# An attention and expert kernel: a reduction, a cast, a key order and the first expert's product are moved

## The chip, the cores and the metric

The kernel runs on one core of a Trainium2 chip. The core has a matmul engine (PE, with its weight loads as PEld), a vector engine (DVE), a scalar engine (ACT), a general engine (POOL), and a sync engine (SP) that issues nearly all DMAs. Each engine works through its own list in order; semaphores hold an instruction until what it reads is there and what it overwrites is free. The metric is the time of one execution on the device, in microseconds, the median of several runs.

## The reference, cut to what matters

```
# u, v: 8 x 2496 x 256, z: 8 x 2496 x 64, float32
scores = (1 / S) * z @ z.T                  # for each batch, symmetric
attn = maximum(scores, 0) ** 2              # symmetric too
x = (u * (attn @ v)).reshape(19968, 256)
logits = x @ w_gate                         # 8 experts
e_of = argmax(logits, axis=1)
gate_w = softmax(logits)[e_of]
for e in range(8):                          # at most 80 rows for each expert
    tok = the 80 rows of largest gate_w among those with e_of == e
    h = maximum(x[tok] @ w1[e], 0)          # w1[e]: 256 x 1024
    out[tok] = gate_w[tok] * (h @ w2[e])    # w2[e]: 1024 x 256, other rows are 0
```

## The kernel before

**Staging.** The kernel goes through 8 batches `b`. A batch is cut into 5 chunks `qc` of 512 queries (the last has 448), and a chunk goes in ten steps `r`, each for a pair of key tiles of 128 rows. A fifth number in a tile name is the pair's first key tile: `al_5_3_12` is batch 5, chunk 3, key tiles 12 and 13. `order(b, qc)` gives the pairs of a chunk. The loop over all steps is written out by hand: what each engine does, and when, is the order of the calls.

**A pair.** A number is carried as a high and a low part, so a product takes three matmuls. Half of the score matrix is computed and the other half is mirrored. For a computed pair PE makes the scores `s` (line 407), ACT takes Relu and Square (lines 409, 410, tile `a`) and casts the high part `ah` (line 114), and DVE subtracts to the low part `al` (line 58) and transposes `a` into a tile `x` (line 316), which SP writes to memory as `y` (line 326). A mirrored pair is read back from there as `blk` (line 343); ACT casts `ah` (line 387) and DVE subtracts `al`. The last pair of a chunk lies on the diagonal; half of it is mirrored through `xd`, `yd` and `md` (lines 352, 360, 369; cast in line 422). `attend_pair` then multiplies `ah` and `al` with the values `vt` into two accumulators `acc`: 24 matmuls on half arrays (line 444). The scores or casts of a pair are issued two steps ahead of its `attend_pair` (`LOOK = 2`).

**The end of a chunk.** ACT copies the accumulators out (`take`, line 516). Over the next chunk's steps DVE adds halves, multiplies with `u` (line 524) and cuts off low parts; PE makes the gate logits `pl` (line 602), and DVE sums them to `lg` (line 609, `chunk_sum`). The steps of this are the table `CHAIN` in `finished`. `pl`, and the count tables `wp` (lines 839 to 841, `blocks`) for the first two batches, use the one buffer with tag `m`, so `wp` can begin only when DVE has read `pl`. The step 9 that calls `blocks` is also the one at which `chunk_sum` is called.

**The next batch's values.** `prep_vh` casts a quarter or so of the values of the next batch to the high part of `vt`, on ACT, at the five places of `V_HIGH`; the last of them is in the last step of a batch.

**The end.** In the last batch the rows for the experts are fetched and spread (`x_at`: `fetch_x`, `spread_x`, line 799), and the first two experts' weights are loaded and split (`LOADS`, `SPLITS`). After the last attention product come the last rows' sums and logits (`chunk_x_last`, lines 538 to 540, `chunk_logits_last`, lines 549 to 553), the gate, and a feed-forward stage of eight experts. For expert i it transposes the rows (`xp_i`, line 1302; split to `xTh_i`, `xTl_i`), multiplies with w1 (`hp_i`, line 1322), takes Relu (line 1325), transposes the result (line 1337; split to `hTh_i`, `hTl_i`) and multiplies with w2 (`op_i`, line 1352).

Of the kernel before, what the change touches and what calls it, by code (L numbers as in the profile page):

```python
# [8 lines left out]
F32 = mybir.dt.float32  # L9
# [10 lines left out]
P = 128  # L20
# [5 lines left out]
def attn_moe_kernel(ctx, tc, zT, uT, v, wg, w1, w2, out, seq, cap):  # L26
# [39 lines left out]

    const = ctx.enter_context(tc.tile_pool(name="const", bufs=1))
    dram = ctx.enter_context(tc.tile_pool(name="dram", bufs=1, space=DRAM))
    NV, NW, NR = 6, 2, 5
    NA = 4  # L70
    NX = 4
    SQ = 32
# [67 lines left out]
    def prep_vh(b, g, raw, e0):  # L140
        vt = vpool.tile([P, QT, 2, D], F32R, tag="vt", name=f"vt_{b}_{g}")
        cp(e0, vt[:, :, 0], raw)
        v_t[b, g] = vt
# [145 lines left out]
    def order(b, qc):  # L289
        rest = [p for p in range(NP) if p // 2 != qc]  # L290
        if whole_block(b, qc):
            return [NP - 2, NP - 1, *range(NP - 2)] if qc == NQ - 2 else list(range(NP))
        if qc == NQ - 2:
            rest = rest[-2:] + rest[:-2]
        return [2 * qc, *rest, 2 * qc + 1]

    pairs_of = {(b, qc): order(b, qc) for b in range(B) for qc in range(NQ)}
# [406 lines left out]
    def count(b, k0, n, slot):  # L704

        kr = RB[b] * BPB + k0
        tp = ps_m.tile([P, 2, CH], F32, tag="m", name=f"tp_{b}_{k0}")[:, :, :n * E]
        rows = [slice(0, P)] if b < 2 else HALVES
        for h in range(2):
            for i, hs in enumerate(rows):  # L710
                nc.tensor.matmul(tp[:, i], ones_b[hs], oh[hs, h, kr:kr + n].rearrange("p k e -> p (k e)"),
                                 start=h == 0, stop=h == 1)
        if b < 2:
            t2 = tot2[:, :, b * BPB:b * BPB + n]
            nc.scalar.copy(out=t2, in_=tp[:, 0].rearrange("p (k e) -> p e k", e=E))
            V.tensor_reduce(out=csum[:, slot], in_=t2, axis=AX.X, op=ALU.add)
        else:
            V.tensor_reduce(out=csum[:, slot], in_=tp.rearrange("p i (k e) -> p e i k", e=E), axis=AX.XY,
                            op=ALU.add)

    def lookup():
# [65 lines left out]
    def fetch_x(g):  # L787
        if not xall:
            xall.append(sqpool.tile([P, E, D], F32, tag="x", name="xall"))
        xg = zpool.tile([P, 2, 2 * D], U16, tag=("zraw", "md")[g % 2], name=f"xg_{g}", bufs=1)  # L790
        for h in range(2):
            gather(xg[:NS, h], xs2.rearrange("(n h) w -> n (h w)", h=2),
                   tok_i[2 * g + h][:NS])
        xg_t[g] = xg

    def spread_x(g):
        xg = xg_t.pop(g)
        for h in range(2):
# [6 lines left out]
    def first_x():  # L805
# [7 lines left out]
        nc.scalar.copy(out=xh, in_=xp[:, :DC * NS])  # L813
        tt(xl, xp[:, :DC * NS], xh, ALU.subtract)

    def both(f, *es):
        for e in es:
            f(e)
# [6 lines left out]
              (3, 3, 8): lambda: both(place_two, 6, 7),  # L825
              (4, 2, 3): tokens,
              (4, 2, 4): lambda: fetch_gates(range(4)), (4, 2, 5): lambda: fetch_gates(range(4, E))}
    x_at = {(NQ - 2, 6): lambda: fetch_x(0), (NQ - 2, 8): lambda: fetch_x(1),
            (NQ - 2, 9): lambda: spread_x(0), (NQ - 1, 0): lambda: (fetch_x(2), spread_x(1)),
            (NQ - 1, 1): lambda: (first_x(), fetch_x(3)), (NQ - 1, 3): lambda: spread_x(2),  # L830
            (NQ - 1, 5): lambda: spread_x(3)}

    def blocks(pool, tag, wpool, src, k0, k1, tab, r0, own="wb"):
        n = (k1 - k0) * E
# [105 lines left out]

    early = [(e, w, part) for e in range(2) for w in (1, 2) for part in range(2)]
    qa, qb, qz = NQ - 3, NQ - 2, NQ - 1
    LOADS = dict(zip([(qa, 6), (qa, 7), (qb, 0), (qb, 2), (qb, 5), (qb, 8), (qz, 2), (qz, 4)], early))
    SPLITS = dict(zip([(qb, 0), (qb, 2), (qb, 5), (qb, 8), (qz, 2), (qz, 4), (qz, 5), (qz, 6)], early))

    RAW = {(qz, 4): (2, 1)}
    WARM = 4, 3
# [18 lines left out]
    def weights_ahead(qc, r):  # L966
        if not places:

            xt, vv = (sqpool, "x"), (vpool, "vt")
            nb = B * NQ * (NQ - 1) // 2  # L970
            a4 = [(apool, f"a{n % NA}") for n in range(nb - NA, nb)]
            late["kept"] = [a4[0]]
            places.extend([xt, xt, xt, vv, a4[1], vv, a4[2], vv, a4[3], vv])
            places.extend([vv, None, None, vv, a4[0], 1])
        if (qc, r) in SPLITS:
            p = SPLITS[qc, r]
            split_w(*p, w_raw.pop(p), V)
        if qc == NQ - 1 and r >= NP - 2:
            split_hi(*kept[r - NP + 2][0], kept[r - NP + 2][1])
        if (qc, r) in LOADS:  # L980
            p = LOADS[qc, r]
            w_raw[p] = load_raw(*p)
        if (qc, r) in RAW:
            raw_whole(*RAW[qc, r])
# [12 lines left out]
    def split_rest():  # L997
        p, raw = kept.pop(0)
        split_w(*p, raw, V)

    def finished(b, qc, r):

        at_end = b == B - 1 and qc == NQ - 2
        rest, lo, store, store2, logits, total = (1, 2, 3, 5, 5, 5) if at_end else CHAIN
        if qc == NQ - 1:
            logits, total = 7, 8
        if r == rest:
            chunk_rest(b, qc)
        if r == lo:
            chunk_lo(b, qc)  # L1010
        if r == store:
            chunk_store(b, qc)
        if r == store2:
            chunk_store2(b, qc)
        if r == logits:
            chunk_logits(b, qc)
        if r == total:
            chunk_sum(b, qc)
        if b < B - 1 and qc == NQ - 1 and r == 9:
            gate_top(b, 0, NQ)  # L1020
        elif qc == 0 and b > 0:
            if r == 0:
                gate_exp(b - 1, 0)
            elif r == 2:
                ex_t[b - 1] = gate_near(b - 1, 0)
            elif r == 3:
                gate_rows(b - 1, ex_t.pop(b - 1), gp, V)
                gate_recip(b - 1, gp)
            elif r == 5:
                gate_store(b - 1)  # L1030
                count(b - 1, 0, BPB, b - 1)
            elif r == 9 and b <= 2:
                kr = RB[b - 1] * BPB
                blocks(ps_m, "m", gp, oh, kr, kr + BPB, wtwo, (b - 1) * BPB)
        elif at_end and r == 7:
            gate_top(b, 0, NQ - 1)
        elif at_end and r == 8:
            gate_exp(b, 0)

    ex_t = {}  # L1040
    CHAIN = 3, 5, 4, 6, 7, 9

    with tc.manual_schedule(engines={ET.PE, ET.Activation, ET.DVE, ET.SP, ET.Pool}):
        prep_z(0, 0, raw0)
# [9 lines left out]
        for i, (b, qc, r) in enumerate(steps):  # L1054
# [38 lines left out]
            if b + 1 < B:  # L1093
                for j, load, prep in keys_in[qc]:
                    if r == prep:
                        prep_z(b + 1, j, z_raw.pop((b + 1, j)))
                    if r == load:
                        z_raw[b + 1, j] = load_z(b + 1, j)
                if (qc, r) in V_LOAD:
                    g = V_LOAD.index((qc, r))  # L1100
                    v_raw[b + 1, g] = load_v(b + 1, g)
                if (qc, r) in V_HIGH:
                    g = V_HIGH.index((qc, r))
                    prep_vh(b + 1, g, v_raw[b + 1, g], nc.scalar)
            v_low(b, qc, r)
            if r == 5 and b < B - 1:
                zero_out(b * NQ + qc, B * NQ)
# [16 lines left out]
        x_sum[prev] = chunk_tiles(*prev)  # L1124
        for kk, c in ((3, 0), (2, 0), (3, 1), (1, 0), (2, 1), (1, 1)):
            attend(*prev, NT - kk, c, kk == 1)
            if (kk, c) == (3, 1):
                count(b, 0, BPB - 2, b)
            if kk == 1:
                chunk_x_last(*prev, c)  # L1130
        split_rest()
        gate_near(b, 0)
        chunk_store(*prev)
# [160 lines left out]
    def ffn_of(own, num, expert, tw, to, ps_t, ps_h):  # L1294
# [14 lines left out]

        def ffn1(i, part):  # L1310
            ns = num(i)
            xh, xl = x_t[i]
            w1h, w1l = wt[expert(i), 1]
            if part == 0:
                h_t[i] = tw.tile([P, F], F32, tag="h", name=f"h_{i}{own}")
            f0 = part * 512
            hp = ps_h.tile([P, 512], F32, tag="h", name=f"hp_{i}_{f0}{own}")
            n = 0
            for ops in (((xh, w1h), (xh, w1l)), ((xl, w1h),)):
                for c in range(DC):  # L1320
                    for x, w in ops:
                        nc.tensor.matmul(hp[:ns], x[:, c * ns:(c + 1) * ns], w[:, c, f0:f0 + 512],  # L1322
                                         start=n == 0, stop=n == 3 * DC - 1)
                        n += 1
            nc.scalar.activation(out=h_t[i][:ns, f0:f0 + 512], in_=hp[:ns], func=AF.Relu)

        def ffn_h(i, half):
# [38 lines left out]
    def ahead():  # L1366
        with ExitStack() as stack:
            def pool(name, bufs, **k):
                return stack.enter_context(tc.tile_pool(name=name, bufs=bufs, **k))
# [2 lines left out]
            tl = pool("tl", 1)  # L1372
            tw = pool("tw", 2)
            late["behind"] = to = pool("to", 2)
            ps_t = pool("ps_t", 3, space=PSUM)
            ps_h = pool("ps_h", 4, space=PSUM)
            ps_x = pool("ps_x", 1, space=PSUM)
            ffn_x, ffn1, ffn_h, ffn2, result = ffn_of("", lambda i: NS, lambda i: i, tw, to, ps_t, ps_h)

# [215 lines left out]
```

## Time and profile before

| | |
|---|---|
| median of 3 runs | 1367.61 us (1365.89 to 1367.83) |
| the profiled execution, its own time | 1366.91 us |
| its span in the trace | 1365.2 us |
| PE busy | 1314.5 us, 96% |
| DVE busy | 1056.5 us, 77% |
| ACT busy | 1018.1 us, 75% |
| mean granted clock of PE | 0.992 of full |

A trace is of one execution. Its span is 1.7 us shorter than that execution's time on the device, which has a start and an end outside the trace. Shares of busy time are averages over all stages. Where an engine idles, the profile gives the idle time and the instruction that released it.

### The profile page before, as it was taken

The numbers are of one execution on the slowest core, as the hardware profiler recorded it, in microseconds if no ns is written. First come the engines' busy times: TensorE is split into PE (matmuls) and PEld (weight loads), VectorE is DVE, ScalarE is ACT, GpSimd is POOL, SyncE is SP. The second block draws the span as 40 slices with busy tenths as digits, with TensorE's granted clock in tenths as the row PEclk, the third lists the DMA queues.
The fourth block names the chain that finished last, engine by engine and source line by source line (L and its number), as shares of the span: only waits on it lengthen the run. The fifth ranks groups of instructions, "written<-read, shape, count | busy, mean of one in ns | idle before, by whom it ended". The sixth has DMA issues, their size and how long they took to land.

```text
span 1365.2 us, 31275 instructions
## 1 busy us (share of the span) xinstructions
PE 1314.5 (96%) x13121; PEld 1077.8 (79%) x13121; DVE 1056.5 (77%) x1270; ACT 1018.1 (75%) x1110; POOL 38.5 (3%) x58
## 2 busy tenths in 40 slices
PE   9999999999989999999999999999999999999997
PEld 6887777778778787878788787887888787887786
DVE  8877788667887778877887778867887778877785
ACT  8976688666886668785787668876787758877765
POOL 0000000000000100000001100000000000000111
PEclk9999999899999999999999999999999999999989
DMA  6799968798768858878478786798578695688763
GB/s 212 253 293 232 265 217 248 202 241 226 237 209 220 253 147 256 243 222 245 155 246 259 223 228 199 236 245 235 160 234 259 200 262 162 218 249 250 217 208 128
DMA packets 192739, 306.98 MB, mean 225 GB/s; under 512 B 35872, under 2 KB 117712, under 8 KB 182352
## 3 DMA queue, kind: packets, MB, share of 16 engines
q1 hardware_dynamic: 191312, 302.62, 75.2%
q0 software_dynamic: 1280, 2.30, 0.6%
q8 instruction: 104, 1.70, 0.5%
q14 instruction: 43, 0.35, 0.1%
HBM read 163.66 MB, written 136.09 MB: 220 GB/s over the span
## 4 chain that ended last, share of the span: by engine, by line
PE 60%; ACT 11%; DVE 10%; DMA 9%; issue 6%; SPq 3%; DVEq 0%; POOL 0%; ACTq 0%; POOLq 0%
PE acc L444 47%; PE s L407 8%; DVE al L58 3%; ACT a L409 3%; ACT ah L114 3%; ACT a L410 2%; DVE x L316 2%; DMA md<-yd 2%; DMA vraw<-v 2%; PE hp L1322 2%; ACT xf L516 2%; DMA yd<-xd 1%; DVE xf L58 1%; DMA blk<-y 1%; PE pl L602 1%
## 5 line engine op out<-in xcount | busy, mean ns | idle before, releaser
L444 PE MATMUL acc<-ah,vt 64*128 64x512 f32 (+1 forms) x6240 | 961.6, 385 | 6.9 <-ACT xf L516 5.8
L444 PEld LDWEIGHTS acc<-ah,vt 64*128 64x128 f32 x6240 | 590.8, 185 | 123.0 <-ACT xf L516 19.0
L444 PE MATMUL acc<-al,vt 64*128 64x512 f32 (+1 forms) x3120 | 617.7, 386 | 18.4 <-DVE al L58 17.6
L58 DVE TENSOR_TENSOR al<-a,ah 128x1024 fp32r<-128x1024 f32 (+1 forms) x240 | 270.9, 1129 | 165.3 <-ACT ah L114 163.0
L444 PEld LDWEIGHTS acc<-al,vt 64*128 64x128 f32 x3120 | 302.3, 185 | 89.4 <-DVE al L58 36.6
L409 ACT ACTIVATE a<-s 128x1024 f32<-128x1024 f32 x240 | 229.0, 954 | 140.4 <-PE s L407 113.5
L387 ACT CAST ah<-blk 128x1024 fp32r<-128x1024 f32 x160 | 163.8, 1050 | 116.4 <-PE acc L444 107.5
L410 ACT ACTIVATE a<-a 128x1024 f32<-128x1024 f32 x240 | 238.0, 992 | 7.6
L58 DVE TENSOR_TENSOR al<-blk,ah 128x1024 fp32r<-128x1024 f32 x160 | 194.0, 1222 | 54.5 <-ACT ah L387 54.5
L114 ACT CAST ah<-a 128x1024 fp32r<-128x1024 f32 (+3 forms) x217 | 213.6, 984 | 5.5
L316 DVE STREAM_TRANSPOSE x<-a 128x1024 f32<-128x1024 f32 x160 | 198.0, 1238 | 0.0
L58 DVE TENSOR_TENSOR xf<-xf 128x1024 f32<-128x1024 f32 (+1 forms) x78 | 91.9, 1178 | 0.0
L407 PE MATMUL s<-zh,zl 64*128 64x512 f32 x480 | 89.9, 370 | 0.0
L407 PE MATMUL s<-zl,zh 64*128 64x512 f32 x480 | 89.9, 370 | 0.0
L516 ACT COPY xf<-acc 128x1024 f32<-128x1024 f32 (+1 forms) x78 | 75.5, 992 | 14.0 <-PE acc L444 14.0
L407 PE MATMUL s<-zh,zh 64*128 64x512 f32 x320 | 64.3, 398 | 4.4 <-ACT a L409 4.4
L407 PEld LDWEIGHTS s<-zl,zh 64*128 64x128 f32 x480 | 45.3, 184 | 8.1
L58 DVE TENSOR_TENSOR al<-md,ah 128x512 fp32r<-128x512 f32 x37 | 25.1, 679 | 33.6 <-ACT ah L422 33.6
L407 PEld LDWEIGHTS s<-zh,zl 64*128 64x128 f32 x480 | 45.5, 185 | 6.3
L147 DVE TENSOR_TENSOR vt<-vraw,vt 128x1024 fp32r<-128x1024 f32 x40 | 48.3, 1208 | 0.0
L524 DVE SCALAR_TENSOR_TENSOR xf<-xf,ut 128x1024 f32<-128x1024 f32 (+1 forms) x39 | 46.1, 1181 | 0.0
L58 DVE TENSOR_TENSOR xl<-xf 128x1024 bf16<-128x1024 f32 (+1 forms) x39 | 45.8, 1174 | 0.0
(187 smaller groups left out, 738.3 us busy)
## 6 DMA issues: line engine op xcount, KB each, us to landing
y<-x SPq DMA_DIRECT2D x80, 1024.0 KB
blk<-y SPq DMA_DIRECT2D x320, 256.0 KB
out<-idle SPq DMA_DIRECT2D x40, 512.0 KB
vraw<-v SPq DMA_DIRECT2D x32, 512.0 KB
ut<-uT SPq DMA_DIRECT2D x32, 512.0 KB
wraw<-w SPq DMA_DIRECT2D x30, 512.0 KB
xu<-xf SPq DMA_DIRECT2D x24, 512.0 KB
yd<-xd SPq DMA_DIRECT2D x37, 256.0 KB
```

What stands on the lines that cost most here:

```text
L58: V.tensor_tensor(out=o, in0=a, in1=b, op=op)
L114: eng.copy(out=o, in_=i)
L147: e1.tensor_tensor(out=vt[:, :, 1], in0=raw, in1=vt[:, :, 0], op=ALU.subtract)
L316: V.transpose(out=x[:, :, :, t:t + 2].rearrange("p n k t s -> p t k n s"), in_=a)
L387: nc.scalar.copy(out=natural(ah), in_=src)
L407: nc.tensor.matmul(s[:, h, c0:c1], zk[hs, t * P:(t + 1) * P], zq[hs], start=n == 0, stop=n == 2)
L409: nc.scalar.activation(out=a[:, :, c0:c1], in_=s[:, :, c0:c1], func=AF.Relu)
L410: nc.scalar.activation(out=a[:, :, c0:c1], in_=a[:, :, c0:c1], func=AF.Square)
L444: nc.tensor.matmul(acc_t[b, qc][c][:, h, :nq], v_t[b, k // QT][hs, k % QT, iv, c * P:(c + 1) * P], x[hs, k % 2, :nq], start=at not in begu ...
L516: nc.scalar.copy(out=x[:, :, c], in_=acc_t[b, qc][c][:, :, :x.shape[-1]])
L524: V.scalar_tensor_tensor(out=x[:, 0], in0=x[:, 0], scalar=CSQ, in1=u_t[b, qc][:, :, :x.shape[-1]], op0=ALU.mult, op1=ALU.mult)
L1322: nc.tensor.matmul(hp[:ns], x[:, c * ns:(c + 1) * ns], w[:, c, f0:f0 + 512], start=n == 0, stop=n == 3 * DC - 1)
```

## The change

It has six parts. (1) `chunk_sum` comes at step 8 in place of 9; with it some numbers of the last batch's chain. (2) In the fourth chunk (`qc == 3`) of all batches but the last, the pairs are taken as 6, 0, 8, 9, 1, ... in place of 6, 8, 9, 0, 1, ..., by first key tile 12, 0, 16, 18, 2, ... in place of 12, 16, 18, 0, 2, .... (3) The fifth of the casts in `V_HIGH` goes from ACT (line 114) to DVE (line 116). (4) In the last batch, rows are fetched and spread in chunk 3 in place of chunk 4, and loads and splits of weights get other steps. (5) The first expert's w1 product is issued behind the last attention product, into the buffer of the scores, with one Relu for both halves; `count` follows it, in one slice of 128 rows in place of two of 64. (6) Buffers: one more weight buffer, and other places for two weight tiles; two pools of accumulators change places.

```diff
-    NV, NW, NR = 6, 2, 5
+    NV, NW, NR = 6, 3, 5
...
         if qc == NQ - 2:
-            rest = rest[-2:] + rest[:-2]
+            rest = rest[:1] + rest[-2:] + rest[1:-2]
         return [2 * qc, *rest, 2 * qc + 1]
...
-        rows = [slice(0, P)] if b < 2 else HALVES
+        rows = [slice(0, P)] if b < 2 or b == B - 1 else HALVES
...
+    def first_product():
+        hp = ps_s.tile([P, 2, CH], F32, tag="s", name="hp_first")
+        h = vpool.tile([P, QT * 2 * D], F32, tag="vt", name="h_first")
+        for part in range(2):
+            product1(hp[:, part], 0, 0, part, NS)
+        nc.scalar.activation(out=h[:NS, :F], in_=hp[:NS].rearrange("p a f -> p (a f)"), func=AF.Relu)
+        return h[:, :F]
+
+    def product1(hp, i, e, part, ns):
+        xh, xl = x_t[i]
+        w1h, w1l = wt[e, 1]
+        f0 = part * 512
+        n = 0
+        for ops in (((xh, w1h), (xh, w1l)), ((xl, w1h),)):
+            for c in range(DC):
+                for x, w in ops:
+                    nc.tensor.matmul(hp[:ns], x[:, c * ns:(c + 1) * ns], w[:, c, f0:f0 + 512],
+                                     start=n == 0, stop=n == 3 * DC - 1)
+                    n += 1
...
-    x_at = {(NQ - 2, 6): lambda: fetch_x(0), (NQ - 2, 8): lambda: fetch_x(1),
-            (NQ - 2, 9): lambda: spread_x(0), (NQ - 1, 0): lambda: (fetch_x(2), spread_x(1)),
-            (NQ - 1, 1): lambda: (first_x(), fetch_x(3)), (NQ - 1, 3): lambda: spread_x(2),
-            (NQ - 1, 5): lambda: spread_x(3)}
+    x_at = {(NQ - 2, 0): lambda: fetch_x(0), (NQ - 2, 1): lambda: fetch_x(1),
+            (NQ - 2, 4): lambda: (spread_x(0), fetch_x(2)), (NQ - 2, 5): lambda: (spread_x(1), fetch_x(3)),
+            (NQ - 2, 8): lambda: spread_x(2), (NQ - 2, 9): lambda: spread_x(3), (NQ - 1, 1): first_x}
...
-    LOADS = dict(zip([(qa, 6), (qa, 7), (qb, 0), (qb, 2), (qb, 5), (qb, 8), (qz, 2), (qz, 4)], early))
-    SPLITS = dict(zip([(qb, 0), (qb, 2), (qb, 5), (qb, 8), (qz, 2), (qz, 4), (qz, 5), (qz, 6)], early))
+    LOADS = dict(zip([(qa, 6), (qa, 7), (qb, 0), (qb, 3), (qb, 5), (qb, 7), (qb, 9), (qz, 3)], early))
+    SPLITS = dict(zip([(qb, 2), (qb, 4), (qb, 6), (qb, 7), (qz, 2), (qz, 4), (qz, 5), (qz, 6)], early))
...
-        rest, lo, store, store2, logits, total = (1, 2, 3, 5, 5, 5) if at_end else CHAIN
+        rest, lo, store, store2, logits, total = (1, 3, 3, 5, 5, 6) if at_end else CHAIN
...
-    CHAIN = 3, 5, 4, 6, 7, 9
+    CHAIN = 3, 5, 4, 6, 7, 8
...
-                    prep_vh(b + 1, g, v_raw[b + 1, g], nc.scalar)
+                    prep_vh(b + 1, g, v_raw[b + 1, g], V if g == NQ - 1 else nc.scalar)
...
             attend(*prev, NT - kk, c, kk == 1)
-            if (kk, c) == (3, 1):
-                count(b, 0, BPB - 2, b)
             if kk == 1:
                 chunk_x_last(*prev, c)
+        h_first = first_product()
+        count(b, 0, BPB - 2, b)
         split_rest()
...
             ns = num(i)
-            xh, xl = x_t[i]
-            w1h, w1l = wt[expert(i), 1]
+            if not own and i == 0:
+                h_t[i] = h_first
+                return
```

**Where DVE stands at the step of `blocks`.** The rows are DVE's from the end of batch 1's chunk 1 to the start of chunk 2; `al_1_2_8` and `al_1_2_0` are the low parts of chunk 2's first two pairs, `xd` the quarter that is transposed, `lg` the sum that frees the buffer `m` for `wp`.

```order
 L58 TENSOR_TENSOR al_1_1_6_3315<-a_1_1_6_3304,ah_1_1_6_3314 128x2x256
-L58 TENSOR_TENSOR al_1_2_8_3404<-a_1_2_8_3393,ah_1_2_8_3403 128x1024
-L352 STREAM_TRANSPOSE xd_1_2_3407<-a_1_2_8_3393 128x2x2x4x32
-L58 TENSOR_TENSOR al_1_2_0_3459<-blk_1_2_0_2898,ah_1_2_0_3457 128x1024
-L609 TENSOR_REDUCE lg_1_3461<-pl_1_0_3344 128x32
+L58 TENSOR_TENSOR al_1_2_8_3409<-a_1_2_8_3398,ah_1_2_8_3408 128x1024
+L352 STREAM_TRANSPOSE xd_1_2_3412<-a_1_2_8_3398 128x2x2x4x32
+L609 TENSOR_REDUCE lg_1_3432<-pl_1_0_3344 128x32
+L58 TENSOR_TENSOR al_1_2_0_3466<-blk_1_2_0_2898,ah_1_2_0_3464 128x1024
 L58 TENSOR_TENSOR al_1_2_2_3477<-blk_1_2_0_2898,ah_1_2_2_3475 128x1024
```

The sum stood behind the low part of the second pair and now stands ahead of it, right behind the transpose.

**The start of batch 6.** These are ACT's rows around the first computed pairs of batch 6 (`a_6_0_4`, `a_6_0_6`), with the copies of batch 5's last accumulators (`xf_5_4`) between; `vt_6_4` is the last part of the values.

```order
-L516 COPY xf_5_4_13764<-acc_5_4_0_13380 128x2x448
-L516 COPY xf_5_4_13764<-acc_5_4_1_13381 128x2x448
-L114 CAST ah_6_0_4_13774<-a_6_0_4_13742 128x1024
-L114 CAST vt_6_4_13781<-vraw_6_4_13601 128x4x256
+L409 ACTIVATE a_6_0_4_13743<-s_6_0_4_13744 128x1024
+L410 ACTIVATE a_6_0_4_13743<-a_6_0_4_13743 128x1024
+L516 COPY xf_5_4_13765<-acc_5_4_0_13380 128x2x448
+L516 COPY xf_5_4_13765<-acc_5_4_1_13381 128x2x448
+L114 CAST ah_6_0_4_13775<-a_6_0_4_13743 128x1024
 L409 ACTIVATE a_6_0_6_13783<-s_6_0_6_13784 128x1024
 L410 ACTIVATE a_6_0_6_13783<-a_6_0_6_13783 128x1024
```

The cast of `vt_6_4` stood ahead of the Relu that reads `s_6_0_6`; that Relu now follows the cast of `ah_6_0_4` directly. On DVE the cast stands ahead of `al_6_0_6`, and the sum `lg` that stood there has moved up.

**Chunk 3 of batch 5 on DVE.** First the rows before, from the chunk's first pair on; `xf_5_2` is the chain of the chunk before.

```order
L58 TENSOR_TENSOR al_5_3_12_12881<-a_5_3_12_12870,ah_5_3_12_12880 128x1024
L352 STREAM_TRANSPOSE xd_5_3_12884<-a_5_3_12_12870 128x2x2x4x32
L58 TENSOR_TENSOR al_5_3_16_12955<-a_5_3_16_12916,ah_5_3_16_12954 128x1024
L316 STREAM_TRANSPOSE x_5_4_3_12958<-a_5_3_16_12916 128x2x4x4x32
L609 TENSOR_REDUCE lg_5_12502<-pl_5_1_12821 128x32
L58 TENSOR_TENSOR al_5_3_18_12972<-a_5_3_18_12961,ah_5_3_18_12971 128x1024
L316 STREAM_TRANSPOSE x_5_4_3_12958<-a_5_3_18_12961 128x2x4x4x32
L58 TENSOR_TENSOR xf_5_2_12938<-xf_5_2_12938 128x1024
L58 TENSOR_TENSOR al_5_3_0_13007<-blk_5_3_0_12504,ah_5_3_0_13005 128x1024
L524 SCALAR_TENSOR_TENSOR xf_5_2_12938<-xf_5_2_12938,ut_5_2_12692 128x1024
L58 TENSOR_TENSOR al_5_3_2_13038<-blk_5_3_0_12504,ah_5_3_2_13036 128x1024
```

The same stretch of the change:

```order
L58 TENSOR_TENSOR al_5_3_12_12881<-a_5_3_12_12870,ah_5_3_12_12880 128x1024
L352 STREAM_TRANSPOSE xd_5_3_12884<-a_5_3_12_12870 128x2x2x4x32
L609 TENSOR_REDUCE lg_5_12473<-pl_5_1_12821 128x32
L58 TENSOR_TENSOR al_5_3_0_12947<-blk_5_3_0_12434,ah_5_3_0_12945 128x1024
L58 TENSOR_TENSOR al_5_3_16_12960<-a_5_3_16_12949,ah_5_3_16_12959 128x1024
L316 STREAM_TRANSPOSE x_5_4_3_12963<-a_5_3_16_12949 128x2x4x4x32
L58 TENSOR_TENSOR xf_5_2_12929<-xf_5_2_12929 128x1024
L58 TENSOR_TENSOR al_5_3_18_13005<-a_5_3_18_12994,ah_5_3_18_13004 128x1024
L316 STREAM_TRANSPOSE x_5_4_3_12963<-a_5_3_18_12994 128x2x4x4x32
L524 SCALAR_TENSOR_TENSOR xf_5_2_12929<-xf_5_2_12929,ut_5_2_12692 128x1024
L58 TENSOR_TENSOR al_5_3_2_13038<-blk_5_3_0_12434,ah_5_3_2_13036 128x1024
```

`al_5_3_0` has gone from the ninth row to the fourth; up to `al_5_3_2` DVE has the same eleven instructions in both.

## Rows read from the trace of the kernel before

**Rows 1.** The page: busy us of each engine, share of the span, instructions.

```profile
PE 1314.5 (96%) x13121; PEld 1077.8 (79%) x13121; DVE 1056.5 (77%) x1270; ACT 1018.1 (75%) x1110; POOL 38.5 (3%) x58
```

**Rows 2.** Waits of PE: who waited for whom, us in total, times, longest.

```profile
PE acc L444 <- DVE al L58: 17.6, 26, 2.3
...
PE s L407 <- ACT a L409: 5.5, 8, 1.1
```

**Rows 3.** Timeline of PE: start, duration, instruction, idle before; batches 1 and 2.

```profile
237.79 0.39 PE L444 MATMUL acc<-al,vt 64*128 64x512 f32 x2
241.85 0.30 PE L839 MATMUL wp<-upper,oh 128*80 128x128 bf16 x1 [3.67 <-DVE lg L609]
...
248.47 0.62 PE L444 MATMUL acc<-ah,vt 64*128 64x512 f32 x4
...
249.16 0.62 PE L444 MATMUL acc<-ah,vt 64*128 64x512 f32 x4
...
407.72 0.25 PE L839 MATMUL wp<-upper,oh 128*80 128x128 bf16 x1 [3.58 <-DVE lg L609]
...
412.46 0.62 PE L444 MATMUL acc<-ah,vt 64*128 64x512 f32 x4
```

**Rows 4.** Timeline of DVE, the same place of batch 1.

```profile
237.83 0.71 DVE L352 STREAM_TRANSPOSE xd<-a 128x512 f32<-128x512 f32 x1
240.21 1.23 DVE L58 TENSOR_TENSOR al<-blk,ah 128x1024 fp32r<-128x1024 f32 x1 [1.66 <-ACT ah L387]
241.35 0.35 DVE L609 TENSOR_REDUCE lg<-pl 128x32 f32<-128x192 f32 x1
```

**Rows 5.** Windows: busy time of PE, PEld, DVE, ACT, POOL, granted clock, DMA share, GB/s.

```profile
237.00:272.00 35.00, 31.33 (x297) 25.89 (x295) 22.55 (x23) 21.41 (x24) 0.00 (x0) 0.90 0.78 212
...
1299.00:1306.50 7.50, 6.37 (x22) 4.93 (x22) 4.88 (x17) 2.32 (x4) 1.07 (x4) 0.54 0.25 90
```

**Rows 6.** Timeline of ACT, start of batch 6.

```profile
980.18 1.06 ACT L114 CAST vt<-vraw 128x1024 fp32r<-128x1024 f32 x1
```

**Rows 7.** Timeline of PE, start of batch 6.

```profile
982.21 0.50 PE L407 MATMUL s<-zh,zh 64*128 64x512 f32 x2 [0.57 <-ACT a L409]
...
990.84 0.50 PE L444 MATMUL acc<-al,vt 64*128 64x512 f32 x2 [0.41 <-DVE al L58]
```

**Rows 8.** Timeline of DVE, start of batch 6.

```profile
982.62 0.32 DVE L609 TENSOR_REDUCE lg<-pl 128x32 f32<-128x192 f32 x1
984.37 1.23 DVE L58 TENSOR_TENSOR al<-a,ah 128x1024 fp32r<-128x1024 f32 x1 [1.42 <-ACT ah L114]
...
988.77 0.69 DVE L116 CAST ah<-a 128x1024 fp32r<-128x1024 f32 x1
```

**Rows 9.** Timeline of PE, chunk 3 of batch 5.

```profile
929.83 0.51 PE L444 MATMUL acc<-al,vt 64*128 64x512 f32 x2 [1.06 <-DVE al L58]
```

**Rows 10.** Timeline of DVE, chunk 3 of batch 5.

```profile
930.83 2.35 DVE L58 TENSOR_TENSOR al<-blk,ah 128x1024 fp32r<-128x1024 f32 x2
```

**Rows 11.** Waits of ACT.

```profile
ACT ah L422 <- DMA md<-yd: 21.5, 8, 3.6
```

**Rows 12.** Timeline of SP, its DMA issues in chunk 3 of batch 5.

```profile
932.07 1.75 SPq L343 DMA_DIRECT2D blk<-y  x4
933.86 0.44 SPq L326 DMA_DIRECT2D y<-x  x1
...
934.82 3.78 SPq L369 DMA_DIRECT2D md<-yd  x4
```

**Rows 13.** Timeline of PE, last batch and first experts.

```profile
1281.92 0.47 PE L444 MATMUL acc<-al,vt 64*128 64x448 f32 x2 [0.71 <-DVE al L58]
...
1301.53 0.74 PE L1322 MATMUL hp<-w1h,x_first 128*112 128x512 f32 x1 [1.06 <-DVE d_last L58]
...
1317.15 0.28 PE L1352 MATMUL op<-w2h,hTh 128*112 128x256 f32 x1
```

**Rows 14.** Timeline of DVE, first experts.

```profile
1304.81 0.39 DVE L116 CAST xTh<-xp 128x224 fp32r<-128x224 f32 x1 [1.88 <-PE xp L1302]
```

More of the change, by code (lines that the diff above doesn't have):

```diff
@@ L717, in count @@
         else:
-            V.tensor_reduce(out=csum[:, slot], in_=tp.rearrange("p i (k e) -> p e i k", e=E), axis=AX.XY,
+            V.tensor_reduce(out=csum[:, slot], in_=tp[:, :len(rows)].rearrange("p i (k e) -> p e i k", e=E), axis=AX.XY,
                             op=ALU.add)
@@ L973, in weights_ahead @@
             places.extend([xt, xt, xt, vv, a4[1], vv, a4[2], vv, a4[3], vv])
-            places.extend([vv, None, None, vv, a4[0], 1])
+            places.extend([None, None, None, vv, a4[0], 1])
         if (qc, r) in SPLITS:
@@ L1317, in ffn1 @@
             hp = ps_h.tile([P, 512], F32, tag="h", name=f"hp_{i}_{f0}{own}")
[L1318 to L1324, printed above, removed]
+            product1(hp, i, expert(i), part, ns)
             nc.scalar.activation(out=h_t[i][:ns, f0:f0 + 512], in_=hp[:ns], func=AF.Relu)
@@ L1374, in ahead @@
             late["behind"] = to = pool("to", 2)
+            ps_h = pool("ps_h", 4, space=PSUM)
             ps_t = pool("ps_t", 3, space=PSUM)
-            ps_h = pool("ps_h", 4, space=PSUM)
             ps_x = pool("ps_x", 1, space=PSUM)
```

## The prediction

> **What bounds the kernel now.** I read the list of waits first, then the timelines where they lie, then the clock by windows. PE is busy for 1314.5 us, 96% of the span [rows 1], so what can be won is in its idle time and in what a lowered clock costs. The list of PE's waits [rows 2] says who ends that idle time: above all DVE, with a low part `al` (26 times, 17.6 us), then ACT, with the Relu that frees the buffer of the scores (8 times, 5.5 us). The timelines show that most of it repeats at fixed places: at each of seven batch starts, and at the third step of chunk 3 in seven batches. Two waits are larger, 3.67 and 3.58 us, ahead of `wp` in batches 1 and 2 [rows 3]. Behind the first of them the same six attention matmuls take twice as long: the window around it has a granted clock of 0.90 [rows 5], a mean of 2.4 and 1.2 GHz. The other place with the lower clock is the start of the experts: 0.54 of full between 1299.0 and 1306.5 [rows 5].
>
> The sum is made against the profiled execution: span 1365.2 us, own time 1366.9, 0.7 below the median. A change of under 0.2% (2.7 us) would not be told from none by a measurement of this kernel.
>
> **Part 1, the sum a step sooner: 9.8 us.** Before, `wp` waits for `lg`, which DVE has in its list behind `al_1_2_0`; that one waits for ACT's cast until 240.21, so `lg` runs at 241.35, though the transpose `xd` ended at 238.54 [rows 4]. Afterwards `lg` stands directly behind `xd`. DVE starts an instruction some 0.08 before the one ahead ends (240.21 + 1.23 against 241.35), so `lg` runs from 238.45 to 238.80, and `wp`, which came 0.15 behind its end (241.70 to 241.85), at 238.95: 2.90 sooner. PE stops at 238.18 (237.79 + 0.39), so 0.77 of the wait stays. Batch 2 has the same order and a wait shorter by 0.09; I take 2.8. Together 5.7. What is late next: `al_1_2_0` moves behind a sum of 0.35 that has 1.66 of idle time to run in, so nothing.
>
> Then the clock. From `wp` at 241.85 to the row at 248.47 lie three thin matmuls (0.3: each lasts 0.25 to 0.30 and they overlap) and five groups of six, each 0.69 at full clock (248.47 to 249.16): 6.62 less 0.3 less 3.45 leaves 2.9. In batch 2: 412.46 less 407.72 is 4.74, less 0.3 and four groups (2.76) leaves 1.7 [rows 3]. A PE that is this much sooner meets the `al` of its next pairs, so I take 4.1 of the 4.6. Would a wait of 0.77 still lower the clock? Chunk 3 has waits of 1.06 [rows 9], and PE has one of 2.3 [rows 2]; the only windows with a lowered clock are those of [rows 5], batch 2's and the very end. So the clock stays. Ends: 5.7 if it falls all the same, 10.3.
>
> **Part 3, the last cast of the values on DVE: 6.3 us.** At a batch start the score matmul waits for the Relu that reads the buffer before it (0.57 at 982.21 [rows 7]), and that Relu stands behind the cast of `vt` on ACT, 1.06 long [rows 6]. Of the eight such waits (5.5) one, 1.1 long, is at the kernel's start, so the seven sum to 4.4. Without the cast the Relu comes 0.95 sooner (the 1.06 less an overlap of 0.1) and the wait goes. Eight microseconds on PE waits again, 0.41 for `al` at 990.84 [rows 7]; that sums to 2.8 over seven. DVE works from 984.37 to there without idle, so this goes only as far as DVE starts sooner. The cast costs DVE 0.69, as the same shape does at 988.77, and lies in the 1.42 of idle time ahead of 984.37 [rows 8]. From the sum's end, less the overlap, about 982.87, the cast lasts to 983.5; `al_6_0_6` then starts 0.87 sooner, at an `ah` that comes 0.95 sooner. PE wants 0.57 + 0.41 = 0.98 and gets 0.87: 6.1, and a little more where the first wait is 0.86 in place of 0.57. I take 6.3. Ends: 4.4 (only the first wait goes) and 7.2. Should the cover be missing, the cast costs what it lasts, 0.69.
>
> **Part 2, the order of chunk 3: 3.2 us.** PE waits 1.06 for `al_5_3_0` at 929.83 [rows 9], and in each of the seven batches within 0.04 of it: 7.4. Three computed pairs in a row have put that low part behind two transposes and a sum. The new order interleaves a mirrored pair. But DVE has the same instructions up to `al_5_3_2` in both, and finishes it at 932.0 (930.83 and half of 2.35) [rows 10]; going through the new list with the durations of the old one it ends at 931.8. PE without its wait would ask for it at about 931.5. So 0.3 is left, and some 0.8 is won by the middle of the chunk.
>
> It is not all kept, since ACT waits for `md` near the end of the same chunk: 21.5 us, eight times, up to 3.6 [rows 11]. SP gets to `md` at 934.82, behind a `blk`, a `y` and a `vraw`, and all four are issued only from 932.07, when `al_5_3_2` has freed a buffer [rows 12]. `al_5_3_2` ends 0.25 sooner, so `md` lands about 0.25 sooner, not 0.8, and the casts and copies behind it, which the next chunk's first pairs need, are as late. Where they have no slack (batches 4 and 6) I count 0.25, where a little (0, 1, 2) 0.35, where more (3, 5) 0.8: 3.2. Ends: 0 and 5.6.
>
> Here a rule bears on it. The Trainium skill, DMA: Bandwidth & Descriptors, section Queues, rings and completion order, has descriptors taken in ring order on each DMA engine of an issuing engine's one queue. By that rule `md` cannot pass the transfers ahead of it, and a faster PE alone brings nothing forward; a sum that trusted it wholly would put part 2 at 1.8 (0.25 in each batch). The trace agrees in order: `md` is issued last and landed last.
>
> **Part 4, the last batch: 1.1 us.** The wait of 0.71 at 1281.92 [rows 13] has a split of weights and a low part `xl` ahead of the `al` on DVE, and one of 0.37 in chunk 3 (among the 26) likewise; in the change both splits stand behind. The spreads move between chunks, on ACT. Ends: 0 and 1.5.
>
> **Parts 5 and 6, the first product: 1.2 us.** Before, twelve `hp_0` matmuls begin at 1301.53 behind a wait of 1.06 for the gate [rows 13] and run at the lower clock [rows 5]. Afterwards they stand ahead of the last logits, at full clock some 2.8 us (at 0.23 each, a third of a group of six that runs two at a time). The logits then end some 2.5 later, but `xp_1` no longer stands behind six of the twelve. By my replay `d_last` is 1.1 later, `xp_1` comes at 1302.3 and `xTh_1` at 1302.9 in place of 1304.81. DVE's idle time ahead of it is 1.88 [rows 14], and from there DVE is nearly full up to the second expert's `op` at 1317.15 [rows 13]. So at most 1.9 can be won. If the clock falls again in the thin logits, six matmuls of `hp_1` cost 1.4 more. I take 1.2; ends -1 and 1.9.
>
> A rule speaks against this part. The Trainium skill, TensorE: Matmul & The Clock Gate, Part 1, calls the lower clock the default and says that activity releases it. By that rule sixteen logits of 8 columns and the gate behind them, which stay, would lower it again, and part 5 gives about nothing. The trace has such a fall at 1299.3, directly after such matmuls; no run here shows the other order.
>
> **Sum.** 9.8 + 6.3 + 3.2 + 1.1 + 1.2 = 21.6, so 1366.9 - 21.6 = 1345.3 us.
>
> **Rivals.**
> - `md` decides more. It lands as late as before and the second wait at batch starts stays too: parts 2 and 3 give 0 and 4.4, so 1366.9 - 16.5 = 1350.4. For it: [rows 11]. Against: SP's list has the same transfers ahead of `md`. Chance 0.15.
> - Chunk 3 gives all it can. If `md` has slack, part 2 is 5.6 and part 3 is 7.2: 1342.0. Chance 0.13.
> - The sum moves but the clock still falls behind the shorter wait in both batches: 4.1 less, 1349.4. If something else than `lg` holds `wp`, all 9.8 is gone: 1355.1. Against: `lg` ends 0.15 ahead of `wp` both times. Chance 0.08.
> - The clock falls again at the first experts, hand in hand with the thin logits: 1.2 less to 2.2 less, about 1347. Chance 0.15.
> - Slower: `y` now stands between `vraw` and `md` and waits for the transposes of the pair 18, which have moved back. SP reaches it at 933.86 [rows 12] and the transpose should end near 930. If it came later, all behind it on SP would wait, `md` first, and PE by as much in each of seven batches. It decides from 21.6 / 7 = 3.1 us of delay at `md`, so with the transpose at 937; a delay of 4 gives 1373. Chance 0.03.
> - The forecast, 1344 to 1347: 0.46.
>
> **Range and chances.** The range goes from full gains everywhere (10.3 + 7.2 + 5.6 + 1.5 + 1.9 = 26.5, 1340.4) and a margin of one, 1339, to the lower ends of two or three parts together (8 + 4.4 + 1 + 0.5 + 0 = 13.9), 1353. Faster by over 0.2%: 0.94; within it: 0.03; slower: 0.03.
>
> **What would show it.** Part 1: `wp` in batches 1 and 2 with a wait under 1 us, and the clock at full there. Part 3: no wait for the Relu at batch starts, and 0.1 to 0.2 for `al` eight microseconds on. Part 2: the wait of 1.06 gone, one of some 0.3 a pair later; ACT's waits for `md` longer by half a microsecond, about 25 us in all. Parts 5 and 6: `op_1` 1 to 2 us nearer to the last attention product. What would make it wrong: a wait that I have not seen in the 26 others for `al`, since a PE that is sooner meets DVE at places where it now just does not.

## The result, and the profile after

The change takes 1342.64 us (1340.64 to 1343.44) against 1367.16 us; the ratio is 0.982, with a 95% interval of 0.9803 to 0.9837. It is faster by 1.8%, 24.5 us, inside the stated range and beyond the forecast of 21.6. The profiled execution's span is 1341.7 us, 23.5 less than before.

First the page of the change, its line on the engines, which answers to [rows 1]:

```profile
PE 1304.5 (97%) x13119; PEld 1071.5 (80%) x13119; DVE 1060.9 (79%) x1277; ACT 1014.0 (76%) x1102; POOL 43.3 (3%) x58
```

PE's busy time falls too, in part because no matmul of batches 1 and 2 runs at the lower clock now (the window below). Then the waits of PE, the answer to [rows 2]:

```profile
PE acc L444 <- DVE al L58: 16.5, 24, 3.0
PE acc L444 <- ACT xf L516: 5.3, 11, 0.8
...
PE wp L858 <- DVE lg L609: 1.3, 2, 0.7
PE s L407 <- ACT a L409: 1.1, 1, 1.1
PE pl L549 <- DVE csum L718: 0.9, 1, 0.9
PE xp L1321 <- DVE d_last L58: 0.6, 1, 0.6
PE hp L832 <- DVE oh L638: 0.6, 1, 0.6
```

The two waits for `lg` are 0.7 each in place of 3.6, and the seven waits for the Relu are gone; the one at the kernel's start is left. The waits for `al` have hardly shrunk, from 17.6 to 16.5. The forecast wanted far less there, so the first thing to read is where they stand. PE's timeline at the place of `wp` in batch 1, at a batch start, and in chunk 3 of batch 5 (answers to [rows 3, 7, 9]):

```profile
238.27 0.25 PE L858 MATMUL wp<-upper,oh 128*80 128x128 bf16 x1 [0.66 <-DVE lg L609]
...
971.60 0.50 PE L444 MATMUL acc<-al,vt 64*128 64x512 f32 x2 [0.32 <-DVE al L58]
...
914.29 0.50 PE L444 MATMUL acc<-al,vt 64*128 64x512 f32 x2 [1.07 <-DVE al L58]
```

The wait of 1.06 in chunk 3 is as long as it was. It comes 12.7 us behind the chunk's first attention product (901.59) and not 9.6 (929.83 less 920.21): it is now the fifth pair's, `al_5_3_2`, and no longer the fourth's, `al_5_3_0`. The same holds in all seven batches. DVE shows what went on there (the answer to [rows 10]):

```profile
903.10 1.23 DVE L58 TENSOR_TENSOR al<-blk,ah 128x1024 fp32r<-128x1024 f32 x1 [1.43 <-ACT ah L387]
906.21 1.23 DVE L58 TENSOR_TENSOR al<-a,ah 128x1024 fp32r<-128x1024 f32 x1 [1.88 <-ACT ah L114]
...
911.91 1.19 DVE L524 SCALAR_TENSOR_TENSOR xf<-xf,ut 128x1024 f32<-128x1024 f32 x1
913.01 2.35 DVE L58 TENSOR_TENSOR al<-blk,ah 128x1024 fp32r<-128x1024 f32 x2
```

DVE idles for 1.43 and 1.88 us before its second and third low parts, both times for a cast on ACT. Then it works without a break, the chain of the chunk before included, and reaches `al_5_3_2` at 913.01. ACT's timeline of the same stretch:

```profile
899.75 1.02 ACT L516 COPY xf<-acc 128x1024 f32<-128x1024 f32 x1 [0.20 <-PE acc L444]
901.11 1.01 ACT L516 COPY xf<-acc 128x1024 f32<-128x1024 f32 x1 [0.34 <-PE acc L444]
902.02 1.05 ACT L387 CAST ah<-blk 128x1024 fp32r<-128x1024 f32 x1
902.97 1.03 ACT L409 ACTIVATE a<-s 128x1024 f32<-128x1024 f32 x1
```

The Relu of the pair 16 runs at 902.97, behind two copies of accumulators and a cast, 1.4 behind the chunk's start. Before, it ran ahead of the copies. As the third pair and no longer the second, it is issued a step later.

Last, the windows of the change, one around `wp` in batch 1 and two at the first experts (columns as in [rows 5]), and PE's timeline at the first experts (answers to [rows 13]).

```profile
237.00:272.00 35.00, 34.34 (x349) 28.00 (x347) 24.16 (x27) 26.55 (x30) 0.00 (x0) 1.00 0.99 253
```

```profile
1272.00:1279.40 7.40, 5.98 (x41) 4.59 (x39) 5.22 (x17) 5.17 (x9) 0.00 (x0) 1.00 0.86 329
1279.40:1286.30 6.90, 6.25 (x25) 4.88 (x26) 6.22 (x15) 2.82 (x6) 2.84 (x4) 0.51 0.20 54
```

```profile
1272.63 0.36 PE L444 MATMUL acc<-ah,vt 64*128 64x448 f32 x1
1272.92 0.48 PE L832 MATMUL hp_first<-w1h,x_first 128*112 128x512 f32 x1
...
1276.92 0.18 PE L549 MATMUL pl<-idle 128*128 128x32 bf16 x1 [0.89 <-DVE csum L718]
1276.94 1.93 PE L553 MATMUL pl<-wg_sb,xf 128*128 128x8 f32 x16
1279.47 0.60 PE L1321 MATMUL xp<-ident,xall 112*128 112x112 f32 x2 [0.60 <-DVE d_last L58]
...
1293.78 0.28 PE L1366 MATMUL op<-w2h,hTh 128*112 128x256 f32 x1
```

Around `wp` the granted clock is 1.00, before it was 0.90 [rows 5]. The first product runs at full clock where it was put. The lower clock begins at 1279.4, behind the sixteen thin logits, and lasts as long as before, 6.8 us (before from 1299.3). The second expert's second product comes 21.1 us (1293.78 less 1272.63) behind the last attention product, as before (1317.15 less 1296.02).

### The profile page after: what moved, and what is told of

It reads as the page before. It is cut to its first block, busy times and chain, and to the rows that moved or that the text cites. A ratio compares the mean times of both kernels' runs of the same rounds, so it can differ in the third digit from the quotient of the medians.

```text
span 1341.7 us, 31268 instructions
## 1 busy us (share of the span) xinstructions
PE 1304.5 (97%) x13119; PEld 1071.5 (80%) x13119; DVE 1060.9 (79%) x1277; ACT 1014.0 (76%) x1102; POOL 43.3 (3%) x58
## 4 chain that ended last, share of the span: by engine, by line
PE 72%; DVE 8%; ACT 7%; DMA 7%; issue 4%; SPq 2%; POOL 0%; DVEq 0%; ACTq 0%; POOLq 0%
PE acc L444 57%; PE s L407 9%; DVE al L58 3%; DMA blk<-y 2%; ACT a L409 2%; DVE x L316 2%; ACT ah L114 2%; PE hp L832 1%; PE pl L602 1%; DMA md<-yd 1%; ACT a L410 1%; PE op L1366 1%; DMA zraw<-zT 1%; DVE xf L58 1%; ACT ah L387 1%
## 5 line engine op out<-in xcount | busy, mean ns | idle before, releaser
L444 PE MATMUL acc<-al,vt 64*128 64x512 f32 (+1 forms) x3120 | 614.4, 385 | 17.1 <-DVE al L58 16.5
```

The lines of the kernel that those rows point to most:

```text
L444: nc.tensor.matmul(acc_t[b, qc][c][:, h, :nq], v_t[b, k // QT][hs, k % QT, iv, c * P:(c + 1) * P], x[hs, k % 2, :nq], start=at not in begu ...
```

## The experiments

In each, the ratio is that to the kernel before, measured along with it on the same chip. 0.1% is 1.4 us. Spans are not compared with those of the two traces above: in chunk 2 of batch 4 all ten traces are 2.4 to 5.1 us longer than before's or the change's, whichever has the same order of pairs there, whatever else was edited, and no run shows why. e5 to e10 stand here for their times alone, not as kernels to use.

**The parts alone.** Four kernels, each with one group of edits.

```diff
e1:  -    CHAIN = 3, 5, 4, 6, 7, 9
     +    CHAIN = 3, 5, 4, 6, 7, 8
e2:  -            rest = rest[-2:] + rest[:-2]
     +            rest = rest[:1] + rest[-2:] + rest[1:-2]
e3:  -   prep_vh(b + 1, g, v_raw[b + 1, g], nc.scalar)
     +   prep_vh(b + 1, g, v_raw[b + 1, g], V if g == NQ - 1 else nc.scalar)
e4:  the whole change without these three
```

> The kernel before with the sum at step 8 in place of 9 and nothing else. If the sum's place in DVE's list holds the count table and the clock falls only behind a wait as long as 3.6 us: two waits of some 0.7, full clock there, 9.8 to 10.4 us less than before, about 1357. Rival, the clock falls behind the shorter wait too: 5.7 less, about 1361.5. Rival, something else holds the table's buffer: no change.

Measured: 1359.01 against 1369.79, ratio 0.9924 (0.9909 to 0.994), 10.4 us of 1367. Its waits of PE:

```profile
PE wp L839 <- DVE lg L609: 1.3, 2, 0.7
```

And its window around the first of them:

```profile
237.00:272.00 35.00, 34.25 (x345) 27.75 (x345) 23.68 (x25) 27.14 (x30) 0.00 (x0) 1.00 0.95 237
```

The waits for `lg` are 0.7 each and the clock does not fall there (1.00). Both rivals are out; the sum's place in DVE's list held `wp`.

> The kernel before with the new order of chunk 3 and nothing else. The forecast's step: the wait of 1.06 for al at the chunk's third step goes, one of 0.3 is left, 3.2 less. What the trace of the whole change suggests: the wait keeps its 1.06 and moves to a pair further on, since ACT's Relu of the third pair now stands behind the copies of the accumulators; only small waits at the chunk's start go, 3 to 3.5 less, about 1364. Rival, these small gains need the other parts: within 1 of before.

Measured: 1365.42, ratio 0.9968 (0.9958 to 0.9978), 4.4 us. Its waits of PE:

```profile
PE acc L444 <- DVE al L58: 16.9, 26, 2.6
...
PE acc L444 <- ACT xf L516: 4.8, 10, 0.8
```

The waits for `al` are as many as before, 26, and 0.7 shorter in sum; those for the copies fell from 5.8 to 4.8. So the order wins, and alone, but not by the wait that it seemed made for. The listed waits hold 1.7. Of the rest, some 1.1 would be chunk 2 of batch 4, by an estimate: there the traces with the old order (e1, e3, e4, e8) are 3.4 to 3.6 longer than before's, and this one, with the new order, 2.4 longer than the change's. What is left lies in waits too short to be listed (below).

> The kernel before with the fifth cast of the values on DVE and nothing else. The forecast: seven batch starts of 0.87 each, 6.3 less, 1361. Lower end: only the wait for the Relu goes, 4.4 less, 1363. If waits too short to be listed go as well: 6.8 less, 1360.4.

Measured: 1362.58, ratio 0.9951 (0.9936 to 0.9966), 6.7 us: the forecast's term and what the chunk lengths gave (6.8) are both inside; the lower end, 4.4, is just outside.

> The change without the sum's step of the other chunks, the order of chunk 3 and the cast: only the last batch and the first product are new. Forecast: 1.1 and 1.2, 2.3 less, about 1365. If the first product gives nothing, since the clock falls again, and the last batch gives 2.7: also about 1364.5, but with the second expert's second product as far behind the last attention product as before, 21.1 us.

Measured: 1366.45, ratio 0.9977 (0.9968 to 0.9986), 3.1 us; the second product of the second expert is 20.8 behind the last attention product, so in this trace 0.3 is from the first experts. The trace is of an execution of 1368.88, the longest of its eleven. The four ratios lose 0.76 + 0.32 + 0.49 + 0.23 = 1.80%, and the whole change 1.8%: the parts add up, within intervals of 0.1 to 0.15 each.

**Is it `md`?** The forecast held that a late `md` gives back what chunk 3 wins. e5 reads it earlier in SP's list, ahead of the `blk` that waits.

```diff
-            if r == 3 and not whole_block(b, qc):
+            if r == (1 if qc == NQ - 2 else 3) and not whole_block(b, qc):
                 quarter_back(b, qc)
```

> The change with md of chunk 3 read back at step 1 in place of 3, so that its DMAs stand on SP ahead of the blk that waits for al_2. If the late md sets when chunk 4 starts: ACT's waits for md fall from 24.4 us to under 5, and the waits of 0.3 to 0.5 at the start of chunk 4 go in six batches, 2 to 2.5 less than the change, about 1340. Rival, ACT's copies and casts at the chunk's turn set it whatever md does: ACT's waits for md fall too, and the time is within 0.5 of the change.

Measured: 1346.75 against 1368.96, ratio 0.9835 (0.9816 to 0.9854), not better than the change. First three rows of ACT's waits, then of ACT's and PE's timelines at the start of chunk 4 of batch 5:

```profile
ACT xf L516 <- PE acc L444: 22.0, 57, 1.0
...
ACT ah L387 <- DMA blk<-y: 6.8, 4, 2.6
...
ACT ah L422 <- DMA md<-yd: 1.3, 2, 0.6
```

```profile
925.38 0.60 ACT L422 CAST ah<-md 128x512 fp32r<-128x512 f32 x1
...
928.35 1.03 ACT L409 ACTIVATE a<-s 128x1024 f32<-128x1024 f32 x1 [1.84 <-PE s L407]
...
932.43 1.02 ACT L516 COPY xf<-acc 128x1024 f32<-128x1024 f32 x1 [0.99 <-PE acc L444]
```

```profile
937.07 0.47 PE L444 MATMUL acc<-al,vt 64*128 64x448 f32 x2 [0.30 <-DVE al L58]
```

Of ACT's waits for `md`, 24.4 us in the change, 1.3 are left. ACT now waits for PE at these places, and the 0.30 of PE at the start of chunk 4 stays. The rival was right: ACT's waits for `md` were time that it had to spare.

**Is it DVE's list?** e6 leaves the order and lets the chain of chunk 2 come two steps later in chunk 3, so that `al_5_3_2` stands ahead of it.

```diff
-            if r == 0 and prev:
+            held = 2 if qc == NQ - 2 and b < B - 1 else 0
+            if r == held and prev:
                 chunk_add(*prev)
-            if r == (0 if last else 1) and prev:
+            if r == (0 if last else 1 + held) and prev:
                 chunk_x(*prev)
```

> The change with the sum and the product of the chain of chunk 2 called at steps 2 and 3 of chunk 3 in place of 0 and 1, so that DVE has al_2 ahead of both. If DVE's list is what holds al_2 in chunk 3: the wait of 1.06 goes in all seven batches, and md is issued 1.4 sooner, 7 us less than the change, about 1335.5. Rival, ACT's cast or md gives it back at the start of chunk 4: 2 to 4 less. Rival, the wait only moves to al_4 or al_6, behind which the chain now stands: no change.

Measured: 1335.53, ratio 0.976 (0.974 to 0.978): 0.6% or 8 us less than the change, the shortest time of all. PE's waits, and DVE in chunk 3 of batch 5:

```profile
PE acc L444 <- DVE al L58: 8.4, 17, 3.0
```

```profile
905.79 1.24 DVE L316 STREAM_TRANSPOSE x<-a 128x1024 f32<-128x1024 f32 x1
906.95 1.18 DVE L58 TENSOR_TENSOR al<-blk,ah 128x1024 fp32r<-128x1024 f32 x1
908.05 1.21 DVE L58 TENSOR_TENSOR xf<-xf 128x1024 f32<-128x1024 f32 x1
```

Seven waits and 8.1 us are gone from the list; 7.4 of them are the seven waits of chunk 3. `al_5_3_2` directly follows the last transpose. Nothing gives it back at the start of chunk 4: in batch 5 the wait there is 0.32 in both traces. So the chain's two instructions, 2.3 us of DVE ahead of a low part that PE is to read, were what kept the 1.06.

**The clock at the first experts.** e7 adds idle matmuls, whose output nothing reads.

```diff
         count(b, 0, BPB - 2, b)
+        wm = ps_a.tile([P, 2, CH], F32, tag="acc", name="warm_end")
+        for i in range(4):
+            nc.tensor.matmul(wm[:, 0], idle[:, :P], idle, start=True, stop=True)
...
         chunk_logits_last(*prev)
+        for i in range(3):
+            nc.tensor.matmul(wm[:, 1], idle[:, :P], idle, start=True, stop=True)
```

> The change with four idle matmuls of 512 columns behind the count and three behind the last logits, which write to a buffer that nothing reads. If the clock at the first experts falls since PE does little there, and the lower clock is what part 5 loses: it stays at full or falls later, and 1.5 to 3 us are won, about 1340. Rival, DVE's splits set the second expert's product, so that it comes as late at either clock: within 0.7 of the change.

Measured: 1345.48, ratio 0.9827 (0.9805 to 0.9848), no better than the change. Its windows:

```profile
1279.00:1286.90 7.90, 7.14 (x44) 4.76 (x41) 6.00 (x20) 4.87 (x9) 0.00 (x0) 1.00 0.70 271
1286.90:1290.30 3.40, 3.40 (x11) 2.58 (x12) 3.40 (x8) 0.49 (x1) 1.65 (x2) 0.50 0.02 5
```

Here the lower clock began 8.0 us behind the last attention product, not 6.8, and lasted 3.4 us in place of 6.8; the second product came 20.1 behind. But in e5, e6 and e8, without idle matmuls, it also began 7.6 to 8.2 behind and lasted 3.4, with 19.8 to 20.0. So in its trace the idle matmuls did nothing that chance had not done, and how long the lower clock lasts is worth 1.0 to 1.4 us there. DVE's splits do not set that product alone: the expectation's rival is out in the traces.

Two things stay open. The trace of e7 is of an execution of 1348.64 that has two more stretches at the lower clock, 3.4 us each, in batches 0 and 4. And one execution, not traced, had a mean granted clock of 0.999, the highest of all here, so that by an estimate from its span it had at most 4.0 us at the lower clock, about what the end of the kernel alone takes in the traces (3.5 to 5.6); it took 1344.43, no less than the 1344.03 of one with 0.997. So the idle matmuls may at times hold the clock; that this wins time is not shown.

**The order undone, the first product undone.** e8 is the change with the old order of chunk 3; e10 the change with the first product back behind the gate.

```diff
e8:  -            rest = rest[:1] + rest[-2:] + rest[1:-2]
     +            rest = rest[-2:] + rest[:-2]
e10: -        h_first = first_product()
     -            if not own and i == 0:
     -                h_t[i] = h_first
     -                return
```

> The change with the old order of chunk 3. If the order's gain is its own, as alone (4.4 of 1369.8): 4 more than the change, about 1346.7. Rival, the other parts have taken what it wins, or it is bound by md: within 1 of the change.

Measured: 1351.18, ratio 0.9859 (0.9839 to 0.9879), 5.3 us behind the change. The order's gain is its own. A part of the 5.3 is the clock: the traced execution, 1351.24, ran 3.4 us of batch 0 at half clock (last section), and the two of its five with a mean clock of 0.997 took 1348.6 and 1349.1, some 4.5 behind.

> The change with the first expert's product back in its place behind the gate, everything else as in the change. Forecast: 1.2 more than the change. If its worth hangs on when the clock falls: the second expert's second product 21 us behind the last attention product, as before, against 19.8 to 21.1 with the first product moved, so 0 to 1.3 more. Rival, only the move fills PE while it waits for the gate: 2 or more.

Measured: 1348.43, ratio 0.9849 (0.983 to 0.9868), 4.0 behind the change; its second product is 23.7 behind the last attention product. PE there, and the window:

```profile
1278.81 0.74 PE L832 MATMUL hp<-w1h,x_first 128*112 128x512 f32 x1 [3.30 <-DVE xf L58]
```

```profile
1278.00:1288.40 10.40, 9.59 (x32) 7.70 (x33) 6.23 (x21) 3.10 (x6) 0.42 (x1) 0.51 0.24 90
```

The 4.0 lies in the rival's "2 or more", but not for its reason. PE idles 3.3 us, the clock is low for ten, and the logits now stand behind three matmuls of `hp_0`. `hp_0` waited 1.06 for the gate before and is now released by the last sums of `xf`, which read the accumulators. The change had swapped the pools of `hp` and `tp`, so this is not the kernel before's arrangement; that `hp` got the accumulators' place is argued from this release and was not tried. What it shows: the pools as the change has them want the product moved, and the move then repays 2.6 to 3.9 us (23.7 less the 21.1 to 19.8 of the traces that have it). Against the arrangement of before it repaid nothing in the trace of the change, and about 1.0 in the mean of the traces (below).

**The parts without the last batch.** e9 is the kernel before with e1's, e2's, e3's and e6's edits.

> The kernel before with the sum a step sooner, the order of chunk 3, the cast on DVE and the held chain of chunk 3, and the last batch and the first experts as before. If the parts add up: 10.4 and 6.8 as alone, the order and the held chain together 11, against before 28 less, a ratio of 0.9795 to 0.98, with the last batch's 3 still missing. Rival, the held chain needs the last batch's steps: 21 less, 0.985.

Measured: 1341.3 against 1368.91, ratio 0.9794 (0.978 to 0.9809), as the sum of parts has it. The held chain needs nothing from the last batch.

## Why the prediction was right or wrong

**The time was right,** and the terms sum to within 3 us of it. It lies just below the band with the largest chance, 1344 to 1347, and next to the rival in which chunk 3 gives all it can (1342.0), but that rival's gain, the wait in chunk 3, did not come. The trace gives each term by the length of the chunks it lies in: 10.4 for part 1, 6.8 for part 3 and 2.7 for the last batch, which leaves 3.6 of the 23.5 for the order.

**Part 1, forecast 9.8: right.** The waits left are 0.66 and 0.65 (0.77 was forecast), and the chunks around them lose 10.4. The clock stays at full behind them: the lower clock was all due to the longer wait.

**Part 3, forecast 6.3: right, 6.7 measured.** The step that said that 0.1 would be left at `al_6_0_8` did not hold: 0.32 is left. PE comes to that wait 0.84 sooner and not 0.57, since the listed idle time leaves out the overlap of matmul ends: from the start ahead (981.25) to the one at 982.21 it is 0.96, elsewhere 0.23, and the start behind is another 0.11 late. PE gets through the wait as much sooner as DVE does, 0.93 (0.87 was forecast).

**Part 2, forecast 3.2, 3.6 in the trace and 4.4 alone: the size near by luck, both steps wrong.** "Going through the new list with the durations of the old one it ends at 931.8" failed, which is 11.6 behind the chunk's first attention product; it ended 12.6 behind. I had kept ACT's list as it was, but a pair that is taken one place later has its Relu one step later, here behind two copies and a cast. So the wait went to the next pair at its full length. The second step, that a late `md` gives back the win at the start of chunk 4, fell with e5. The two errors cancelled: no wait went, and there was nothing to give back. What the order does win lies in starts. Without that Relu ahead of them the copies free the accumulators sooner: the first copy begins 1.84 ahead of the chunk's first attention product (899.75 to 901.59), before it was 1.05 (919.16 to 920.21). The rows of before, ACT's and PE's, and PE's of the change:

```profile
919.16 1.91 ACT L516 COPY xf<-acc 128x1024 f32<-128x1024 f32 x2
```

```profile
919.73 0.39 PE L407 MATMUL s<-zl,zh 64*128 64x512 f32 x2
920.21 0.73 PE L444 MATMUL acc<-ah,vt 64*128 64x512 f32 x4
```

```profile
901.36 0.39 PE L407 MATMUL s<-zl,zh 64*128 64x512 f32 x2
901.59 0.62 PE L444 MATMUL acc<-ah,vt 64*128 64x512 f32 x4
```

The first attention product came 0.48 behind the scores' last start and now comes 0.23 behind it. It and the low part of the third pair no longer wait some 0.2 each, which the idle times do not list, as the modelled ends of matmuls overlap; in start-to-start times chunks 2 and 3 of batch 5 are 0.6 shorter together. Batch 2 wins 2 us and batch 0 none; batch 2's part includes a wait of 0.9 in its chunk 4 which is not there after. e3, with the old order, has lost it too, so it is not the order's.

**Part 4, forecast 1.1: right in kind, too small.** The two waits for `al` have gone, 0.37 and 0.71, but chunks 3 and 4 of the last batch are 1.0 and 1.7 shorter, 2.7 together. In chunk 4 a wait of 0.42 for `oh` and the matmuls of `count` behind it have gone too, since `count` now follows the first product; the sum had no term for that. What else shortens chunk 3 was not tried.

**Parts 5 and 6, forecast 1.2: not in the trace of the change, about 1.0 in the mean of the traces.** The rival with the clock came true in the change: behind the thin logits it fell for as long as before, and `op_1` kept its distance of 21.1. In e5 to e8 the fall was shorter, and 1.0 to 1.4 was won. The five traces with the old arrangement (before, e1, e2, e3, e9) have `op_1` 20.9 to 21.8 behind the last attention product, 21.3 in the mean; the six with the product moved (the change, e4 to e8) 19.8 to 21.1, 20.3 in the mean. So the term was near, and the trace of the change alone misleads. The Trainium skill, TensorE: Matmul & The Clock Gate, Part 1, says that activity releases the default lower clock. The traces agree in that all twelve have the lower clock at the first experts, for 3.4 to 10.2 us; that part 5 would then give nothing holds for the trace of the change and not for the mean.

**The slower rival** did not come: SP's `y` was not late.

## What to carry to other kernels

When a unit of work changes its place in an order, replay every engine that serves it, not only the one that the wait names: the stage ahead can fall behind other work, and the wait can then move to the next unit at full length, as it did here. A wait of an engine for a DMA is a cost only if that engine is the one the bound engine waits for; the test is to take it away, as e5 did. Where an engine reaches an urgent result behind a chain that nobody needs yet, move the chain: in e6 that was worth 8 us, where the order alone had given 4.4. And one trace does not settle what a stage with a changing clock is worth: compare several.

## What the runs showed of the hardware that was not expected

Waits of the same length do not always lower the clock, and a shorter one can. In batch 0 PE waits 3.04 us at 161.66 in the change, and the clock behind it is at full; in e8 it waits 3.00 at 161.80, and from 162.9 it is at half; in e7 it waits 2.20 at 160.82, and the clock is at half from 160.5. The rows of PE in the change, in e8 and in e7:

```profile
161.66 0.47 PE L444 MATMUL acc<-al,vt 64*128 64x448 f32 x2 [3.04 <-DVE al L58]
```

```profile
161.80 0.47 PE L444 MATMUL acc<-al,vt 64*128 64x448 f32 x2 [3.00 <-DVE al L58]
```

```profile
160.82 0.74 PE L444 MATMUL acc<-al,vt 64*128 64x448 f32 x2 [2.20 <-DVE al L58]
```

The windows of the change, of e8 and of e7 at these places:

```profile
161.60:165.00 3.40, 3.34 (x74) 2.94 (x76) 3.40 (x5) 1.46 (x3) 0.00 (x0) 1.00 0.76 138
```

```profile
162.90:166.30 3.40, 3.40 (x64) 2.74 (x64) 3.33 (x4) 0.19 (x1) 0.00 (x0) 0.50 0.85 224
```

```profile
160.40:163.80 3.40, 2.98 (x16) 2.70 (x18) 3.40 (x4) 1.74 (x3) 0.00 (x0) 0.51 0.79 148
```

Over the twelve traces the wait at this place is 1.8 to 3.0 us long. The clock fell there in e3 (2.88), e7, e8 and e9 (2.41), each time for 3.4 us, and not in the other eight, e6 with 3.01 and the kernel before with 2.31 among them. So a wait of 2.3 that left the clock alone, on which the forecast rested, was weaker evidence than it looked; the 0.7 that was left at `wp` is far from all of these, and in no trace of a kernel with the earlier sum did the clock fall behind `wp`.
